# A long convolution and expert kernel: channels in four parts of 32 instead of two of 64, the first transform in fp32 on two row groups, and the spectra copied to SBUF before they are multiplied

## The chip, the cores and the metric

One core of a Trainium2 chip runs the whole program. The time is device microseconds of one execution; the number reported for a kernel is the median of several executions.

## The reference, cut to what matters

```
def _attn_ref(x, v, pos_emb, w1, w2):            # x, v: (4, 11456, 128)
    h_filt = (np.maximum(pos_emb @ w1, 0.0) @ w2) * np.exp(-0.01 * pos)[:, None]
    u = x * v
    L = 2 * S
    y = irfft(rfft(u, n=L, axis=1) * rfft(h_filt, n=L, axis=0)[None], n=L, axis=1)[:, :S]
    return x * y

def _moe_ref(x, w_skip, w_gate, w1, w2):         # x: the rows of the above, 45824 x 128
    # rows with x @ w_skip > 0 go through one of 8 experts (128 -> 1024 -> 128),
    # chosen by argmax of x @ w_gate and scaled by its softmax; the others stay x
```

So: a product of x and v, a causal convolution of 11456 positions with a filter that a small network makes, a product with x, and then for some rows one expert of eight.

## The kernel before, in words

The sequence is cut into three blocks of 3840 = 60 x 64 positions (NB = 3). Each block is transformed in two stages: a first transform of length 60 (matrix c1) and a second of length 64 (matrices c2, one for each of 60 frequencies). Spectra of the blocks of data are multiplied with spectra of the blocks of the filter, and blocks of the result get the sum of the pairs that belong to them: six products of [128, 1024] for two frequencies of 64 channels, and three sums of that size. Then c3 and c4 take the result back.

The program has four stages, in the order in which they run:

1. `first_phase` (L318). It loads x and v, multiplies them on DVE (`First.mult`, L209), splits the product into two fp32r parts (`First.split`, L215 on ACT and L216 on DVE) and multiplies them with c1 in three products of 512 columns (`First.first`, L204); ACT copies each result out of PSUM (L205), and the ACT queue stores it to the DRAM tensor x1d (L239). c1 is laid out as [120, 2, 120], half of it zeros, so that one of two positions in a tile is used per product. 25 of 48 such steps are done here, the half of the channels that comes first and one more. Between the steps runs the filter (`filt`, L244 to L315): the network, then its first transform (L290), stored to x1d by the POOL queue (L298).
2. `freq_phase` (L356). 60 iterations, each with two frequencies of 64 channels. SP loads c2 (L395) and x1 (L397). PE multiplies the filter's part with c2 (L403, tile t), ACT copies it into gc (L409, four copies), and DVE and POOL make the combined filter g from gc (L410, L411). PE multiplies the data with c2 (L428, tile xp in PSUM); DVE multiplies xp, straight from PSUM, with gc or g (`mult`, L422, six in an iteration); POOL adds the partial products (`add`, L424, three in an iteration). Two iterations later PE multiplies y with c3 (L455), ACT copies zps to z (L456), and SP stores z to the DRAM tensor zd (L460). The 23 remaining steps of the first transform are put between these by `second` and `step` (L371 to L386), in plain fp32 products. The order is written out by hand and each engine runs its instructions in that order.
3. `out_phase` (L1005). SP loads zt from zd (L1060) and a piece of x (L1049); PE multiplies zt with c4 (L1071), DVE with x (L1072), the rows are stored, routed to experts, and the first expert slots run beside this.
4. `late_slots` (L845): the rest of the expert slots.

Names that the later text uses: t, xp, zps are PSUM tiles; x1, gc, g, y, p, z, zt, ox, u and ur are SBUF tiles; in the trace, tiles of the first transform carry the name wf, since they lie in the buffer that later holds the experts' weights; `SPq` and `ACTq` are DMA queues that these engines issue to.

Of the kernel before, what the change touches and what calls it, by code (L numbers as in the profile page):

```python
# [20 lines left out]
E, F = 8, 1024  # L21
# [6 lines left out]
DH = D // 2  # L28
# [13 lines left out]
AHEAD = 1  # L42
LEAD = 3
PIECES = 1.2
FSTART = 2
FEND = 2
QX = 4
# [26 lines left out]
def tables():  # L74
# [6 lines left out]
    c1 = np.zeros((2, K1, 2, K1, 2))  # L81
    c1f = np.zeros((64, 2, 2, K1, 2))
    for p in range(2):
        c1[p, :, p] = c1f[:K1, p, p] = np.stack([np.cos(th), -np.sin(th)], axis=-1)
# [53 lines left out]
    winp = winp.transpose(1, 0, 2, 3)  # L138
    return {
        "c1": c1.reshape(2 * K1, 2, 2 * K1).astype(f), "c1f": c1f.reshape(128, 2, 2 * K1).astype(f),  # L140
        "c2": c2.astype(f), "c3": c3.astype(f),
# [14 lines left out]
class First:  # L156


    Q = 4
    STEPS = NB * N2 // (2 * Q)  # L160
    XV, US, XS = 3, 2, 3

    def __init__(self, nc, i, x1d, mc, stage):
        self.nc, self.i, self.x1d = nc, i, x1d
        n = self.Q * B * DH
        at = [0]

        def piece(k):
            at[0] += k * n
            return stage[0:2 * K1, at[0] - k * n:at[0]]  # L170
        self.xv = [[piece(1) for _ in range(self.XV)] for _ in "xv"]
        self.us = [piece(1) for _ in range(self.US)]
        self.xs = [piece(2) for _ in range(self.XS)]
        self.c1 = mc.tile([2 * K1, 2, 2 * K1], F32, name="c1")
        nc.scalar.dma_start(self.c1, i["c1"])
        self.tiles, self.loaded, self.parts = {}, 0, {}

    def halves(self, pool):
        self.c1r = pool.tile([2 * K1, 2, 2, 2 * K1], F32R, name="c1r")
        self.nc.scalar.copy(self.c1r[:, 0], self.c1)  # L180
        self.nc.vector.tensor_tensor(self.c1r[:, 1], self.c1, self.c1r[:, 0].bitcast(F32), ALU.subtract)

    def ahead(self, step):

        while self.loaded < min(step + self.XV, 2 * self.STEPS):
            self.load(self.loaded)
            self.loaded += 1

    def load(self, step):
        nc, Q = self.nc, self.Q  # L190
        h, r = divmod(step, self.STEPS)
        blk, ch = divmod(r, N2 // (2 * Q))
        self.tiles[step] = []
        for a, nm in enumerate("xv"):
            t = self.xv[a][step % self.XV]
            nc.sync.dma_start(
                t.rearrange("n (q c) -> n q c", q=Q),
                self.i[nm][ch * 2 * Q:(ch + 1) * 2 * Q, :, blk, h].rearrange("(q p) n b d -> (p n) q (b d)", p=2))
            self.tiles[step].append(t)

    def first(self, xs, terms, pool):
        ps = pool.tile([2 * K1, 512], F32, name="ps")
        for a, (c, rhs) in enumerate(terms):
            self.nc.tensor.matmul(ps, c, rhs, start=(a == 0), stop=(a == len(terms) - 1))  # L204
        self.nc.scalar.copy(xs, ps.rearrange("k (q c) -> k q c", c=B * DH))  # L205

    def mult(self, step):
        if step < 2 * self.STEPS:
            self.nc.vector.tensor_tensor(self.us[step % self.US], *self.tiles.pop(step), ALU.mult)  # L209

    def split(self, step, pool):

        u = self.us[step % self.US]
        ur = pool.tile([2 * K1, 2, self.Q * B * DH], F32R, name="ur")
        self.nc.scalar.copy(ur[:, 0], u)  # L215
        self.nc.vector.tensor_tensor(ur[:, 1], u, ur[:, 0].bitcast(F32), ALU.subtract)  # L216
        self.parts[step] = ur

    def data(self, step, pool):
        nc, Q = self.nc, self.Q  # L220
        h, r = divmod(step, self.STEPS)
        blk, ch = divmod(r, N2 // (2 * Q))
        u = self.us[step % self.US]
        xs = self.xs[step % self.XS]
        n = Q * B * DH
        ur = self.parts.pop(step, None)

        def terms(p, sl):
            if ur is None:
                return (self.c1[:, p, :], u[:, sl]),  # L230
            return [(self.c1r[:, a, p, :], ur[:, b, sl]) for a, b in ((0, 0), (0, 1), (1, 0))]
        for p in range(2):
            for hf in range(n // 512):
                sl = slice(hf * 512, hf * 512 + 512)
                qs = slice(sl.start // (B * DH), sl.stop // (B * DH))
                self.first(xs.rearrange("k (q p c) -> k q p c", q=Q, p=2)[:, qs, p], terms(p, sl), pool)
                if p or hf < n // 512 - 1:
                    yield
        nc.scalar.dma_start(  # L239
            self.x1d[h][:, :, ch * 2 * Q:(ch + 1) * 2 * Q, blk * B * DH:(blk + 1) * B * DH].rearrange("k c m d -> (k c) m d"),  # L240
            xs.rearrange("k (m c) -> k m c", c=B * DH))
        yield

    def filt(self, fc, fp, pool):  # L244
# [7 lines left out]
        c1f = fc.tile([128, 2, 2 * K1], F32, name="c1f")  # L252
# [3 lines left out]
        nc.scalar.dma_start(c1f, i["c1f"])  # L256
# [8 lines left out]
        def positions(blk, k):  # L265

            pt = fp.tile([128, P], F32, name="post", bufs=4)
            for a in range(2):
                at = blk * L + a * HALF + k
                have = max(0, min(P, S - at))  # L270
                rows = slice(a * 64, a * 64 + 64)
                if have < P:
                    nc.vector.memset(pt[rows, have:], 0.0)
                if have:
                    nc.gpsimd.dma_start(pt[rows, :have], i["post"][:, at:at + have])
            return pt
# [10 lines left out]
        def forward(ch, blk, hw, xs):  # L287
            for p in range(2):
                t = pool.tile([2 * K1, M, 2, DH], F32, name="ps")
                nc.tensor.matmul(t, c1f[:, p, :], hw, start=True, stop=True)  # L290
                nc.scalar.copy(xs[p][:, :, :, blk].rearrange("k h m d -> k m h d"), t)
                yield
            if blk < NB - 1:
                return
            for p in range(2):
                n0 = p * H2 + ch * M
                for h in range(2):
                    nc.gpsimd.dma_start(self.x1d[h][:, :, n0:n0 + M, NS * DH:].rearrange("k c m d -> (k c) m d"),  # L298
                                        xs[p][:, h].rearrange("k m s d -> k m (s d)"))
        last = iter(())  # L300
        for ch in range(H2 // M):
            xs = [fp.tile([2 * K1, 2, M, NB, DH], F32, name=f"fx{p}") for p in range(2)]
# [15 lines left out]
def first_phase(tc, fi):  # L318

    with (  # L320
# [5 lines left out]
        fi.halves(fc)  # L326
        f = fi.filt(fc, fp, fps)
        left = 0.0
        pieces = NB * 64 * H2 // 512 + 3 * NB * H2 // 4
        pace = pieces / (4 * (fi.STEPS - FSTART - FEND))  # L330
        END = fi.STEPS + AHEAD
        fi.ahead(0)

        def ready(step):
            if step < END:
                fi.mult(step)
                fi.split(step, fp)
        ready(0)
        for step in range(END):
            for n, _ in enumerate(fi.data(step, fps)):  # L340
                if n == 0:
                    fi.ahead(step + 1)
                    ready(step + 1)
# [7 lines left out]
            if step == fi.STEPS - 1:  # L351
                for _ in f:
                    pass
# [1014 lines left out]
```

## Time and profile before

| what | number |
|---|---|
| median of 3 runs | 1761.56 us (1755.21 to 1770.01) |
| the profiled execution, its own time | 1761.34 us |
| its span, first to last instruction | 1759.6 us |
| mean granted TensorE clock | 0.969 |
| busy share PE, DVE, ACT, POOL | 92%, 72%, 49%, 58% |
| moved by DMA | 357.80 MB, 203 GB/s over the span |
| first_phase | 0 to about 226 us |
| freq_phase | about 226 to 843 us |
| out_phase | about 845 to 1300 us |
| late_slots | about 1300 to 1748 us |

A row of the grouped view names line, engine, operation, what it writes and reads, shapes (partitions x elements) and count; then the busy time in us, the mean of one in ns, and the engine's idle time just before them with what ended it. A row of the view by windows gives, for a stretch of time, the busy time of each engine, the granted clock, the busy share of the 16 DMA engines and what they moved in GB/s. A row of the timeline has start and duration in us. PE runs a plain fp32 product as two instructions, so each such product counts twice in PE's rows.

### The profile page before, as it was taken

Reading aid. Unit: us, or ns where it says so; the run is one execution under the profiler, and the core shown is the slowest. Engines: PE = TensorE matmul, PEld = TensorE weight load, DVE = VectorE, ACT = ScalarE, POOL = GpSimd, SP = SyncE. Lnnn points to the kernel's source line nnn. Section 1 sums busy time; section 2 is a strip of 40 time slices with the busy share of each in tenths; the row PEclk is TensorE's granted clock in tenths of the full one; section 3 lists DMA queues with packets and bytes.
Section 4 is the critical chain, followed back from the end, with each engine's and each line's share of the span. In section 5 each row is a group of like instructions: output and inputs, shape, how many; then the busy total and the mean of one; then the engine's idle time right before and its main releaser. Section 6 shows DMA issues by size and latency. Waiting matters only on the chain. (4 is left out here: it accounts for less than half of the span.)

```text
span 1759.6 us, 27314 instructions
## 1 busy us (share of the span) xinstructions
PE 1615.1 (92%) x8980; PEld 1121.0 (64%) x8980; DVE 1269.8 (72%) x2404; ACT 862.7 (49%) x1582; POOL 1020.3 (58%) x767
## 2 busy tenths in 40 slices
PE   4989679999999799999567999999998999999996
PEld 2556345555556466655234677777677888888996
DVE  3334359777788799999277778767786777777885
ACT  3655435454454344443133555555544555556773
POOL 1111138677678699999002563632657777776874
PEclk9999889999999899999898999999998999999998
DMA  9999999999998599985999888998831111111110
GB/s 246 304 314 304 299 290 277 305 334 301 338 294 239 160 283 302 276 236 147 214 281 257 223 239 233 247 241 227 232 108 47 31 46 46 44 41 33 36 37 21
DMA packets 255122, 357.80 MB, mean 203 GB/s; under 512 B 24961, under 2 KB 189739, under 8 KB 254979
## 3 DMA queue, kind: packets, MB, share of 16 engines
q1 hardware_dynamic: 187692, 269.74, 53.2%
q10 hardware_dynamic: 47687, 47.71, 8.9%
q0 software_dynamic: 19600, 38.59, 8.4%
q8 instruction: 72, 1.18, 0.3%
q14 instruction: 71, 0.58, 0.1%
HBM read 212.91 MB, written 144.02 MB: 203 GB/s over the span
## 5 line engine op out<-in xcount | busy, mean ns | idle before, releaser
L424 POOL TENSOR_TENSOR y<-y,p 128x1024 f32<-128x1024 f32 x120 | 282.9, 2358 | 101.0 <-DVE y L422 96.3
L455 PE MATMUL zps<-y,c 128*128 128x512 f32 x720 | 339.6, 595 | 0.0
L767 POOL DMA_INDIRECT out<-o,ids x186 | 201.6, 1084 | 178.0 <-DVE o L773 128.5
L703 POOL DMA_INDIRECT xt<-out,ids x186 | 199.1, 1070 | 93.1 <-issue 42.5
L422 DVE TENSOR_TENSOR p<-xp,g 128x1024 f32<-128x1024 f32 x180 | 218.4, 1213 | 44.3 <-PE xp L428 27.0
L422 DVE TENSOR_TENSOR y<-xp,gc 128x1024 f32<-128x1024 f32 x180 | 218.5, 1214 | 20.9 <-PE xp L428 20.9
L428 PEld LDWEIGHTS xp<-x,c 128*128 128x128 f32 x720 | 137.6, 192 | 109.5 <-issue 77.2
L871 DVE SCALAR_TENSOR_TENSOR hh<-hp,hh 128x1024 fp32r<-128x1024 f32 x128 | 155.9, 1218 | 70.5 <-ACT hh L870 70.5
L428 PE MATMUL xp<-x,c 128*128 128x256 f32 x720 | 187.9, 384 | 14.1 <-DVE p L422 14.1
L455 PEld LDWEIGHTS zps<-y,c 128*128 128x128 f32 x720 | 134.9, 191 | 99.9 <-issue 89.7
L456 ACT COPY z<-zps 128x512 f32<-128x512 f32 x180 | 104.0, 587 | 189.2 <-PE zps L455 187.2
L669 POOL DMA_INDIRECT ids<-lists,at x93 | 102.7, 1104 | 134.5 <-DMA out<-xm 93.8
L409 ACT COPY gc<-t 64x384 f32<-64x384 f32 x240 | 113.7, 474 | 135.2 <-DVE y L422 80.1
L870 ACT ACTIVATE hh<-hp 128x1024 fp32r<-128x1024 f32 x128 | 132.1, 1032 | 74.2 <-PE hp L763 74.2
L205 ACT COPY wf<-ps 120x512 f32<-120x512 f32 x192 | 110.4, 591 | 83.4 <-PE ps L204 38.5
L738 DVE TENSOR_TENSOR ws<-wf,ws 128x1024 fp32r<-128x1024 f32 x113 | 137.8, 1220 | 18.1 <-ACT ws L733 11.8
L424 POOL TENSOR_TENSOR p<-p,p 128x1024 f32<-128x1024 f32 x60 | 149.5, 2492 | 0.0
L204 PE MATMUL ps<-ur,c1r 120*120 120x512 f32 x300 | 113.3, 508 | 37.9 <-ACT ur L215 20.4
L1071 PE MATMUL y<-zt,c 120*64 120x512 f32 x384 | 108.4, 643 | 32.0 <-DMA zt<-zd 25.9
L833 PEld LDWEIGHTS bank<-wd,h 128*128 128x128 f32 x928 | 107.8, 191 | 30.9 <-issue 30.8
L761 PE MATMUL hp<-hl,ws 128*128 128x512 f32 (+1 forms) x336 | 122.2, 364 | 2.4 <-DVE hh L871 0.9
L733 ACT CAST ws<-wf 128x1024 fp32r x113 | 117.8, 1043 | 10.4 <-issue 5.1
(194 smaller groups left out, 3330.8 us busy)
## 6 DMA issues: line engine op xcount, KB each, us to landing
x<-x1d SPq DMA_DIRECT2D x60, 960.0 KB
x1d<-wf ACTq DMA_DIRECT2D x48, 960.0 KB
zd<-z SPq DMA_DIRECT2D x120, 384.0 KB
zt<-zd SPq DMA_DIRECT2D x96, 480.0 KB
out<-xm SPq DMA_DIRECT2D x96, 258.0 KB
ox<-xo SPq DMA_DIRECT2D x96, 256.0 KB
wf<-x SPq DMA_DIRECT2D x48, 480.0 KB
wf<-v SPq DMA_DIRECT2D x48, 480.0 KB
```

Of the source, the lines that this page charges most:

```text
L409: nc.scalar.copy(gc[h * 64:(h + 1) * 64, a], t[a * 64:(a + 1) * 64])
L422: nc.vector.tensor_tensor(o, x[:, None].broadcast_to([128, 2, B, D]), v[:, :, None, :].broadcast_to([128, 2, B, D]), ALU.mult)
L424: add = lambda o, v: nc.gpsimd.tensor_tensor(o, o, v, ALU.add)
L428: nc.tensor.matmul(x[:, :, k], c2[:, k], x1[:, k, blk * B:(blk + 1) * B, :], start=True, stop=True)
L455: nc.tensor.matmul(zps, c3[:, a, :], y[:, blk, a], start=(a == 0), stop=(a == 1))
L703: ins = nc.gpsimd.indirect_dma_start(out=xt[:, j], out_offset=None, in_=self.rows[0:have], in_offset=bass.IndirectOffsetOnAxis(ap=ids[:, j ...
L733: nc.scalar.copy(w[:, 0], (self.w1f, self.w2f)[which][:, ds(self.where(nc.scalar, tb), F)])
L738: eng.tensor_tensor(w[:, 1], src[:, ds(self.where(eng, tb), F)], w[:, 0].bitcast(F32), ALU.subtract)
L761: nc.tensor.matmul(hp, w[:, 0, c], hl[:, 0], start=True, stop=False)
L767: ins = nc.gpsimd.indirect_dma_start(out=self.rows, out_offset=bass.IndirectOffsetOnAxis(ap=ids[:, j:j + 1], axis=0), in_=o, in_offset=Non ...
L870: nc.scalar.activation(h[:, 0], hp, AF.Relu)
L871: nc.vector.scalar_tensor_tensor(h[:, 1], hp, 0.0, h[:, 0].bitcast(F32), ALU.max, ALU.subtract)
```

## The change

The channels are cut into four parts of 32 (NP = 4), where there were two of 64.

- First transform: x and v come in one tensor xv, laid out beforehand so that a step reads one run of 6144 bytes a partition (two DMAs of 60 partitions). The tile's rows 0 to 59 and 64 to 123 hold two positions; the rows between are cleared once by six memsets. `split` and the fp32r parts are gone: two plain fp32 products of 60 rows and 384 columns, one on rows 0 to 59 of the array and one on rows 64 to 123, write two PSUM banks. c1 is [128, 120] without zeros. The result goes to x1d by the SP queue, one step late, in runs of 6144 bytes. There are 64 steps; 16 of them, one part, run in `first_phase`, and 48 in `freq_phase`.
- Filter: its first transform uses the same two row groups and is stored to a tensor of its own, x1f. The filter's positions are laid out beforehand.
- `freq_phase`: 60 iterations again, each now with four frequencies (KS) of 32 channels. c2 is loaded once, in the first 15 iterations, and stays in SBUF. x1 comes by two DMAs, the data's in runs of 1536 bytes and the filter's in runs of 384 bytes. PE makes data and filter spectra in one product of 480 columns for each frequency, four in an iteration (tile xp, four banks). ACT copies the filter's part to gc as before (four copies), and the data's part to a new SBUF tile xc (two copies). DVE multiplies xc with g: three instructions of 3072, 2048 and 1024 elements where there were six of 1024. POOL adds in two instructions, of 2048 and 1024 elements, where there were three of 1024; g is made in one POOL and one DVE instruction of 384 elements.
- zd has rows of 384 channels' worth of blocks; zt is read from it in runs of 512 bytes where they were of 1024. z is stored at a later place in the iteration.
- The experts' weights are loaded in the last 15 iterations, in another order; some small tiles and their memsets move from `freq_phase` to the start of `out_phase`.

```
-DH = D // 2
+NP = 4
+DH = D // NP
-LEAD = 3
-PIECES = 1.2
+LEAD = 4
+KS = 4
 class First:
-    Q = 4
-    STEPS = NB * N2 // (2 * Q)
+    Q = 2
+    RUN = NS * DH
+    STEPS = N2 // (2 * Q)
+    ALL = NP * STEPS
...
+        for xv in self.xv:
+            for rows in (slice(32, 64), slice(96, 128)):
+                nc.vector.memset(xv[rows], 0.0)
+        self.c1 = mc.tile([128, 2 * K1], F32, name="c1")
...
+        for p in range(2):
+            self.nc.sync.dma_start(self.xv[step % self.XV][p * 64:p * 64 + K1], self.i["xv"][h, ch, p])
...
+            rows = slice(0, 64 + K1)
+            xv = self.xv[step % self.XV][rows]
+            self.nc.vector.tensor_tensor(self.us[step % self.US][rows], xv[:, 0], xv[:, 1], ALU.mult)
...
-            return [(self.c1r[:, a, p, :], ur[:, b, sl]) for a, b in ((0, 0), (0, 1), (1, 0))]
+        for q in range(Q):
+            ps = [pool.tile([2 * K1, 512], F32, name="ps")[:, 0:RUN] for _ in range(2)]
+            for p in range(2):
+                rows = slice(p * 64, p * 64 + K1)
+                nc.tensor.matmul(ps[p], self.c1[rows], u[rows, q * RUN:(q + 1) * RUN], start=True, stop=True)
+            for p in range(2):
+                nc.scalar.copy(xs[:, 2 * q + p], ps[p])
+            if q == 0:
+                self.store()
...
 def freq_phase(...)
+        def step():
+            n = fi.STEPS * fi.Q
+            credit[0] += (n - LEAD) / (NB * (PER - QX)) if done[0] < n else n / (NB * PER)
...
-            x1 = qx.tile([128, 2, NS + NB, DH], F32, name="x1")
-            nc.sync.dma_start(x1, fi.x1d[h][ks].rearrange("k c n (s d) -> (c n) k s d", d=DH))
+            if h == 0:
+                nc.sync.dma_start(c2(ks.start, KS), i["c2"][:, ks.start * 128:ks.stop * 128])
+            x1 = qx.tile([128, KS, (NS + NB) * DH], F32, name="x1")
+            nc.sync.dma_start(x1[:, :, 0:fi.RUN], fi.x1d[h][ks].rearrange("k c n w -> (c n) k w"))
+            nc.sync.dma_start(x1[:, :, fi.RUN:], fi.x1f[ks, :, :, h * w:(h + 1) * w].rearrange("k c n w -> (c n) k w"))
...
+        def spread(n):
+            x1 = xs.pop(n)
+            xp = qpx.tile([128, KS, 512], F32, name="xp")
+            for k in range(KS):
+                nc.tensor.matmul(xp[:, k, 0:(NS + NB) * DH], c2(n % PER * KS + k), x1[:, k], start=True, stop=True)
+            for a in range(2):
+                for h in range(2):
+                    nc.scalar.copy(gc[h * 64:(h + 1) * 64, 1:, a].rearrange("p s k d -> p k s d"), ...)
+            xc = qp.tile([128, NS, KS, DH], F32, name="xc")
+            for k in range(0, KS, 2):
+                nc.scalar.copy(xc[:, :, k:k + 2].rearrange("p s k d -> p k s d"),
+                               xp[:, k:k + 2, 0:NS * DH].rearrange("p k (s d) -> p k s d", d=DH))
+            return xc
...
+            nc.gpsimd.tensor_tensor(g[:, :, 1], v[:, 1:, 1], v[:, 0:NB, 0], ALU.add)
+            nc.vector.tensor_tensor(g[:, :, 0], v[:, 1:, 0], v[:, 0:NB, 1], ALU.subtract)
...
+        def mult(o, xc, g, blk):
+            n = 2 * (NB - blk)
+            x = xc[:, blk * B:(blk + 1) * B].rearrange("p b k d -> p b (k d)")
+            v = g[:, 0:NB - blk].rearrange("p j a d -> p (j a) d")
+            nc.vector.tensor_tensor(o.rearrange("p j a b d -> p (j a) b d"), x[:, None].broadcast_to([128, n, B, D]),
+                                    v[:, :, None, :].broadcast_to([128, n, B, D]), ALU.mult)
...
+            if n + 1 < ALL:
+                xcs[n + 1] = spread(n + 1)
...
+                mult(y, xc, g, 0)
+            back(0)
+            if n < ALL:
+                mult(p1, xc, g, 1)
+            if n + 1 < ALL:
+                gs[n + 1] = filt()
+            store()
+            back(1)
+            if n < ALL:
+                nc.gpsimd.tensor_tensor(y[:, 1:], y[:, 1:], p1, ALU.add)
+                mult(p2, xc, g, 2)
+                nc.gpsimd.tensor_tensor(y[:, 2:], y[:, 2:], p2, ALU.add)
+            back(2)
...
 def out_phase(...)
-            z = ob.tile([2 * K1, 4, BW], F32, name="zt", bufs=ZT)
+            z = ob.tile([2 * K1, 2 * NP, BW], F32, name="zt", bufs=ZT)
             nc.sync.dma_start(z, zs[ch][:, :, blk * BW:(blk + 1) * BW])
```

How the orders of DVE and POOL move in `freq_phase`, one iteration and a half of each. Names: y and p are the products and partial products, xp the spectra in PSUM, xc their copy in SBUF, gc and g the filter's spectra, wf the tiles of the first transform. DVE before:

```order
154 L410 TENSOR_TENSOR g<-gc 128x256
155 L209 TENSOR_TENSOR wf<-wf 120x1024
156 L422 TENSOR_TENSOR y<-xp_1984,gc 128x1024
157 L422 TENSOR_TENSOR p_1960<-xp_1984,g 128x1024
158 L422 TENSOR_TENSOR y<-xp_2007,gc 128x1024
159 L422 TENSOR_TENSOR p_2027<-xp_2029,g 128x1024
160 L422 TENSOR_TENSOR y<-xp_2029,gc 128x1024
161 L422 TENSOR_TENSOR p_2028<-xp_2029,g 128x1024
162 L410 TENSOR_TENSOR g<-gc 128x256
163 L209 TENSOR_TENSOR wf<-wf 120x1024
```

DVE in the change, where L417 is `mult`, L409 is g and L198 is the product of x and v:

```order
118 L409 TENSOR_TENSOR g<-gc 128x3x128
119 L417 TENSOR_TENSOR p_1962<-xc,g 128x1024
120 L198 TENSOR_TENSOR wf<-wf 124x768
121 L417 TENSOR_TENSOR y<-xc,g 128x3072
122 L417 TENSOR_TENSOR p_2018<-xc,g 128x2048
123 L409 TENSOR_TENSOR g<-gc 128x3x128
124 L417 TENSOR_TENSOR p_2019<-xc,g 128x1024
125 L198 TENSOR_TENSOR wf<-wf 124x768
```

In a row of `mult` the first input was xp and is now xc; between two rows of g there were six products of 1024 elements, and there are three, of 1024, 3072 and 2048. POOL before:

```order
61 L411 TENSOR_TENSOR g<-gc 128x256
62 L424 TENSOR_TENSOR y<-y,p_1894 128x1024
63 L424 TENSOR_TENSOR p_1895<-p_1895,p_1894 128x1024
64 L424 TENSOR_TENSOR y<-y,p_1895 128x1024
65 L411 TENSOR_TENSOR g<-gc 128x256
```

POOL in the change, where L408 is g and L473 and L475 are the two sums:

```order
60 L408 TENSOR_TENSOR g<-gc 128x3x128
61 L473 TENSOR_TENSOR y<-y,p_1667 128x2048
62 L475 TENSOR_TENSOR y<-y,p_1668 128x1024
63 L408 TENSOR_TENSOR g<-gc 128x3x128
```

The three sums of 1024 elements became one of 2048 and one of 1024, behind the same instruction that makes g.

More of the change, by code (lines that the diff above doesn't have):

```diff
@@ L219, in data @@
[L219 to L230, printed above, removed]
-            return [(self.c1r[:, a, p, :], ur[:, b, sl]) for a, b in ((0, 0), (0, 1), (1, 0))]
[L232 to L241, printed above, removed]
+        h, ch = divmod(step, self.STEPS)
@@ L400, in filt @@
[L400 to L406 removed]
+            h, k = divmod(n, PER)
+            while done[0] < h * fi.STEPS * fi.Q:
+                next(todo)
+            ks = slice(KS * k, KS * k + KS)
```

312 lines of the change are left out of this document (134 added, 178 removed).

## The prediction

> **What bounds the kernel now.** I read the view by windows first, cut at the stage borders, because the page's shares are means over stages that have different limits.
>
> ```profile
> 0.00:226.00 226.00, 178.32 (x807) 108.97 (x808) 78.72 (x80) 113.26 (x187) 37.66 (x60) 0.93 0.99 293
> 242.00:500.00 258.00, 253.46 (x779) 144.48 (x778) 205.28 (x184) 126.81 (x236) 185.96 (x93) 0.99 1.00 311
> 600.00:840.00 240.00, 239.80 (x780) 143.83 (x779) 239.07 (x210) 98.69 (x191) 220.81 (x112) 1.00 0.81 240
> 855.00:1300.00 445.00, 408.34 (x3623) 282.54 (x3620) 322.05 (x1195) 215.59 (x544) 171.74 (x161) 0.97 0.89 236
> ```
>
> The columns are PE, PEld, DVE, ACT and POOL busy, then clock, DMA share and GB/s. Up to 500 us the DMA engines are full (0.99 and 1.00). From 600 to 840 us PE (239.8 of 240) and DVE (239.1) are both full, and POOL nearly so (220.8). From 855 us on PE leads. The change touches the first 845 us, and zt's reads after that.
>
> Next the groups of 600 to 840 us, a stretch without first transforms:
>
> ```profile
> L424 POOL TENSOR_TENSOR y<-y,p 128x1024 f32<-128x1024 f32 x57 | 134.3, 2357 | 19.2 <-DVE y L422 16.9
> L422 DVE TENSOR_TENSOR y<-xp,gc 128x1024 f32<-128x1024 f32 x83 | 100.4, 1210 | 0.0
> L422 DVE TENSOR_TENSOR p<-xp,g 128x1024 f32<-128x1024 f32 x82 | 99.1, 1209 | 0.0
> L424 POOL TENSOR_TENSOR p<-p,p 128x1024 f32<-128x1024 f32 x28 | 66.2, 2363 | 0.0
> L410 DVE TENSOR_TENSOR g<-gc 128x256 f32<-128x256 f32 x27 | 51.2, 1896 | 0.0
> L411 POOL TENSOR_TENSOR g<-gc 128x256 f32<-128x256 f32 x27 | 24.7, 914 | 0.0
> ```
>
> L410 is the strange row. It has a quarter of the elements of an L422 and takes 1896 ns, longer than the 1210 of L422. The two differ in where they read: L422 has one input in PSUM (xp) and one in SBUF, L410 has both inputs in SBUF. About 28.6 iterations lie in these 240 us, 8.39 us each.
>
> The spread of each such line over the whole run, as minimum, median and maximum in ns:
>
> ```profile
> L410 DVE TENSOR_TENSOR g<-gc x60: 414/1432/1918, 240.2 to 822.6; 128x256 f32<-128x256 f32 x60
> L209 DVE TENSOR_TENSOR wf<-wf x48: 1212/1220/2473, 10.3 to 514.7; 120x1024 f32<-120x1024 f32 x48
> L422 DVE TENSOR_TENSOR y<-xp,gc x180: 1206/1211/1226, 242.4 to 833.5; 128x1024 f32<-128x1024 f32 x180
> L411 POOL TENSOR_TENSOR g<-gc x60: 715/908/966, 240.3 to 824.2; 128x256 f32<-128x256 f32 x60
> L424 POOL TENSOR_TENSOR p<-p,p x60: 2344/2362/3363, 248.6 to 835.1; 128x1024 f32<-128x1024 f32 x60
> ```
>
> L422 never stretches, though POOL adds beside it all the time. L209 and L410, with two SBUF inputs, stretch by up to 1.25 and 1.5 us; so does POOL's L424, by up to 1.0. The timeline shows when (start and duration in us):
>
> ```profile
> 399.23 2.47 DVE L209 TENSOR_TENSOR wf<-wf 120x1024 f32<-120x1024 f32 x1
> ...
> 398.26 2.36 POOL L424 TENSOR_TENSOR y<-y,p 128x1024 f32<-128x1024 f32 x1 [1.97 <-DVE y L422]
> 400.57 3.35 POOL L424 TENSOR_TENSOR p<-p,p 128x1024 f32<-128x1024 f32 x1
> ...
> 623.82 2.35 POOL L424 TENSOR_TENSOR y<-y,p 128x1024 f32<-128x1024 f32 x1
> 626.13 0.91 POOL L411 TENSOR_TENSOR g<-gc 128x256 f32<-128x256 f32 x1
> ...
> 624.55 1.90 DVE L410 TENSOR_TENSOR g<-gc 128x256 f32<-128x256 f32 x1
> ```
>
> POOL's sum ends at 400.62; L209, issued during it, ends at 401.70, 1.08 later; POOL's next sum, issued during L209, ends at 403.92, 2.22 later. Likewise 626.17, then L410 at 626.45 (0.28 later), then L411 at 627.04 (0.59 later). So a DVE instruction with two SBUF inputs and a POOL sum do not run at the same time: each waits for the other's whole instruction. Waiting, each then needs about 0.14 us less than alone, since its start is already done.
>
> **The change part by part. The products.** Today six of the seven DVE instructions of an iteration read xp from PSUM and run beside POOL. In the change all of them read xc and g, both in SBUF, as does the product of x and v, of which 48 now lie in this stage. POOL's elements stay as many. So DVE and POOL, which today work side by side for 8.39 us, would take turns.
>
> Price of a turn, from the four waits above. DVE: 0.28 us for 256 elements and 1.08 for 1024, so 1.04 ns an element and 0.01 fixed: 3072, 2048, 1024 and 384 elements take 3.21 + 2.15 + 1.08 + 0.41 = 6.85 us. POOL: 0.59 for 256 and 2.22 for 1024, so 2.12 ns an element and 0.05 fixed: 2048, 1024 and 384 take 4.39 + 2.22 + 0.86 = 7.47. Together 14.32 us an iteration, the floor, if the other is always waiting when one ends. With the durations alone (DVE 414 and 1220 ns, POOL 715 and 2357 for the same sizes), as if each began after a gap, it is 7.44 + 7.90 = 15.34. The order of both engines shows little reason for a gap: while POOL adds p1, DVE has p2 ready, and while it adds p2, DVE has the next y. I take 14.6. The 48 products of 768 elements add 0.81 each, 39 us (0.95 and 46 at most). The stage from its first product to its last sum: 60 x 14.6 + 39 = 915 us, between 60 x 14.32 + 39 = 898 and 60 x 15.34 + 46 = 966.
>
> Today these two ends are:
>
> ```profile
> 241.28 1.23 DVE L422 TENSOR_TENSOR p<-xp,g 128x1024 f32<-128x1024 f32 x1 [0.61 <-POOL g L411]
> ...
> 837.54 2.36 POOL L424 TENSOR_TENSOR y<-y,p 128x1024 f32<-128x1024 f32 x1
> ```
>
> That is 241.3 to 839.9, 598.6 us.
>
> What lies under the 915 us, and would come out if the turns went away:
>
> ```profile
> L455 PE MATMUL zps<-y,c 128*128 128x512 f32 x720 | 339.6, 595 | 0.0
> L204 PE MATMUL ps<-wf,c 120*120 120x512 f32 x184 | 89.9, 596 | 1.9 <-ACT wf L205 1.8
> L409 ACT COPY gc<-t 64x384 f32<-64x384 f32 x240 | 113.7, 474 | 135.2 <-DVE y L422 80.1 <-PE t L403 35.5 <-PE zps L455 9.3
> L456 ACT COPY z<-zps 128x512 f32<-128x512 f32 x180 | 104.0, 587 | 189.2 <-PE zps L455 187.2 <-ACT gc L409 0.4
> L870 ACT ACTIVATE hh<-hp 128x1024 fp32r<-128x1024 f32 x128 | 132.1, 1032 | 74.2 <-PE hp L763 74.2
> ```
>
> PE streams the same columns as before (4 x 480 = 1920, before 6 x 256 + 2 x 192), in fewer instructions; c3's products stay. At most 60 x 8.39 = 503 us. Of the first transform, L204 gives 89.9 / 184 = 0.49 us a half, 0.98 for 512 columns, so 0.73 for 384: 96 pairs are 70 us if the two row groups run at once, 141 if not (no row shows it). PE needs 573 to 644 of 915. ACT: 4 x 0.474 + 3 x 0.587, two copies to xc of 768 elements between the rows of 512 and 1024, 0.81 each, and 3.2 copies of 384 at 0.47: 6.8 of 14.6 us. xc has two buffers and y three, so PE and ACT work an iteration ahead, and no product stands in line for them. DMA: all loads and stores from the start to zd add up to 227.8 MB, 41.2 of them in the stage before; 186.6 MB in 915 us is 204 GB/s, where 311 was reached. c2 saves 3.9 MB and the long runs some share, both worth nothing here. The 8.4 MB of weights lie in the last 15 iterations, some 218 us.
>
> **The first stage.** It does 16 of 64 steps where it did 25 of 48. Its bytes: 19 loads and 16 stores of 720 KB, 11.8 MB of filter, 3.6 of positions and constants: 41.2 MB, at today's 293 GB/s 141 us. The engines have less to do than that: the fp32r split goes (L215, L216), PE's products become 23 to 47 us beside some 95 of filter. Six memsets stand ahead of the first load and product:
>
> ```profile
> L714 DVE MEMSET xt<- 128x258 f32 x16 | 4.4, 273 | 0.2
> ```
>
> At 1.06 ns an element, 3072 elements take about 3 us; two stand ahead of the first load. I add 4 us: 145. The first product then comes at 145 + 15.3 (241.3 - 226.0) = 160. Bounds: at 311 GB/s 132 + 15 = 147; if PE's and ACT's chains show through, 180.
>
> **zt's reads.** They go from runs of 1024 to runs of 512 bytes.
>
> ```profile
> L1071 PE MATMUL y<-zt,c 120*64 120x512 f32 x384 | 108.4, 643 | 32.0 <-DMA zt<-zd 25.9 <-DVE xm L1131 2.1 <-DVE nt L1149 1.4
> zt<-zd SPq DMA_DIRECT2D x96, 480.0 KB
> q1 hardware_dynamic: 187692, 269.74, 53.2%
> q10 hardware_dynamic: 47687, 47.71, 8.9%
> ```
>
> PE waits for zt 25.9 us in all. The queues' rows give 8.9% of 16 x 1759.6 us over 47687 packets, 52.5 ns for 1000 bytes, and 79.8 ns for 1437: nearly by bytes. zt is 47.2 of the stage's 105 MB (236 GB/s x 445 us), so some 178 of its 396 us of DMA time. If a run of 512 bytes cost half, nothing is added; if it cost as much as 1024, DMA would need 574 us, 129 more than the stage has. By the nearest rows I take 12 us. The Trainium skill, DMA: Bandwidth & Descriptors, section "Why small descriptors are slow (HBM only)", counts three extra cycles for a packet of 32-byte beats; an estimate from that page is 38 cycles for two runs of 512 bytes against 35 for one of 1024, DMA time 411 of 445 us and no loss; no run here shows such reads of zd yet.
>
> **The sum**, against the profiled execution's own 1761.3 us (1.7 more than its span, and 0.2 less than the median of the three runs): the last sum comes at 160 + 915 = 1075 instead of 839.9, +235; zt +12; the tail behind the last sum and the late slots stay. 1761.3 + 247 = **2008 us**. Low ends together (147 + 898, zt 0) give 1966, high ends (180 + 966, zt 40) 2107.
>
> **The rivals.** (1) *No turns: the copy to SBUF costs DVE nothing.* For it: L422 never stretches, and the longer instructions make handing over rarer. Against it: L209 and L410 do stretch, by the length of POOL's instruction, and L424 by the length of L209. Then DMA decides: 186.6 MB at 311 GB/s, 600 us (PE 573, DVE and POOL 7.9 us an iteration at most). The last sum at 760, 80 earlier, zt +12: **1693 us**, faster. It decides if products with two SBUF inputs pass beside sums; each turn that is spared gives back up to 3.2 us. The Trainium skill speaks for this way in VectorE: DVE Perf Modes, section "Rules for kernel authors": for element-wise work on a product's output, stay with PSUM as source or copy to SBUF first if many operations follow; by that rule alone the sum would be the 1693. Its page SBUF — State Buffer, section "Who interferes with whom", speaks against the change: an instruction with two SBUF inputs and a GpSimd instruction that reads SBUF exclude each other; the trace agrees (403.92 and 401.70 above).
>
> (2) *zt becomes the bound*, a run of 512 bytes costing as much as one of 1024: 2008 - 12 + 129 = **2125 us**. Against it: the packets' cost goes by bytes, and PE leads that stage.
>
> (3) *The two row groups do not run at once*, so the change doesn't do what it says. 71 us more on PE, all under the turns: no other time under my forecast. Under (1) PE would need 644 us, and the time were 1737.
>
> **How the numbers follow.** My forecast has 86%: the waiting is in every L410 of the busy stretch. (1) has 8%, (2) 4%, some mixture near no change 2%. The predicted time is 2008 us. The range, 1955 to 2110, is the low and the high end with a little room below; it leaves out (1) and (2). Runs of this kernel spread by 0.8%, so about 1% can be told from no change: faster 0.08, within 1% 0.02, slower 0.90.
>
> **What would show it.** Right: L417 rows well over 3.4, 2.3 and 1.2 us, because their waits count in their durations; POOL's sums over 4.6 and 2.4; DVE and POOL both nearly full in this stage, PE near two thirds; some 14.6 us an iteration; DMA near 200 GB/s; a first product near 160 us. Wrong: L417 near 3.4, 2.3 and 1.2 us while POOL adds, and an iteration near 9 to 10 us with DMA at 1.0; or an out phase much longer than 445 us.

## The result and the profile after

The changed kernel takes 1998.28 us (median of four runs, 1997.51 to 2003.45), the kernel before 1759.90 us (median of four, 1755.21 to 1770.01): a ratio of 1.135, with a 95% interval from 1.130 to 1.141. The forecast was 2008 us. The profiled execution's span went from 1759.6 to 1996.1 us.

First the view by windows of the changed kernel, cut at its own stage borders: the first stage, the frequency stage with and without the last first products, the stage that reads zt. The columns are those of the prediction: PE, PEld, DVE, ACT, POOL busy, clock, DMA share, GB/s.

```profile
0.00:155.00 155.00, 110.21 (x648) 58.76 (x648) 41.67 (x52) 63.25 (x131) 21.14 (x44) 0.89 0.86 267
171.00:800.00 629.00, 499.44 (x1175) 195.96 (x1176) 624.63 (x210) 277.64 (x550) 487.81 (x124) 0.90 0.75 227
800.00:1073.00 273.00, 195.05 (x381) 81.73 (x380) 272.67 (x107) 92.06 (x168) 248.46 (x59) 0.86 0.53 146
1088.00:1536.00 448.00, 410.69 (x3620) 283.13 (x3621) 322.02 (x1195) 215.36 (x544) 172.77 (x161) 0.97 0.93 235
```

In the middle two rows DVE is busy for 624.6 of 629 and 272.7 of 273 us. PE, which was full from 600 to 840 us before, and the DMA engines, which were full up to 500 us, have room (79% and 71% of PE, 0.75 and 0.53 of DMA). A reader who stops here would call DVE the bound and look for work to take off it. The groups of the whole run, with shapes kept apart, say more:

```profile
L427 PE MATMUL zps<-y,c 128*128 128x512 f32 x720 | 404.0, 698 | 124.8 <-ACT z L428 116.9 <-POOL y L473 4.6 <-POOL y L475 3.2
L473 POOL TENSOR_TENSOR y<-y,p 128x2048 f32<-128x2048 f32 x60 | 287.3, 4789 | 68.8 <-DVE p L417 66.5 <-PE ps L215 2.3
L475 POOL TENSOR_TENSOR y<-y,p 128x1024 f32<-128x1024 f32 x60 | 277.9, 4632 | 81.5 <-DVE p L417 78.8 <-DVE first L503 1.2 <-DVE wg L976 1.2
L417 DVE TENSOR_TENSOR p<-xc,g 128x1024 f32<-128x1024 f32 x60 | 264.2, 4403 | 0.0
L417 DVE TENSOR_TENSOR y<-xc,g 128x3072 f32<-128x3072 f32 x60 | 238.8, 3980 | 2.8 <-PE zps L427 1.8 <-ACT xc L400 1.0
L417 DVE TENSOR_TENSOR p<-xc,g 128x2048 f32<-128x2048 f32 x60 | 220.3, 3671 | 0.0
```

The product of 1024 elements costs more (4403 ns) than the one of 3072 (3980). POOL's sum of 1024 (4632) costs nearly as much as that of 2048 (4789). A duration that does not follow the size has a wait inside it. What each one waits for stands in the timeline of one iteration without a first transform, start and duration in us. DVE:

```profile
894.24 5.54 DVE L417 TENSOR_TENSOR p<-xc,g 128x1024 f32<-128x1024 f32 x1
899.70 3.34 DVE L417 TENSOR_TENSOR y<-xc,g 128x3072 f32<-128x3072 f32 x1
902.97 4.43 DVE L417 TENSOR_TENSOR p<-xc,g 128x2048 f32<-128x2048 f32 x1
907.32 1.34 DVE L409 TENSOR_TENSOR g<-gc 128x384 f32<-128x384 f32 x1
908.59 5.52 DVE L417 TENSOR_TENSOR p<-xc,g 128x1024 f32<-128x1024 f32 x1
914.03 3.35 DVE L417 TENSOR_TENSOR y<-xc,g 128x3072 f32<-128x3072 f32 x1
```

POOL in the same stretch:

```profile
893.86 4.83 POOL L473 TENSOR_TENSOR y<-y,p 128x2048 f32<-128x2048 f32 x1
899.92 5.33 POOL L475 TENSOR_TENSOR y<-y,p 128x1024 f32<-128x1024 f32 x1 [1.23 <-DVE p L417]
905.21 3.04 POOL L408 TENSOR_TENSOR g<-gc 128x384 f32<-128x384 f32 x1
908.21 4.82 POOL L473 TENSOR_TENSOR y<-y,p 128x2048 f32<-128x2048 f32 x1
```

Start plus duration is the end of each. Put in one row, the ends are: p of 1024 at 899.78, y at 903.04 (3.26 later), the sum of 1024 at 905.25 (2.21 later), p of 2048 at 907.40 (2.15), POOL's half of g at 908.25 (0.85), DVE's half at 908.66 (0.41), the sum of 2048 at 913.03 (4.37), the next p of 1024 at 914.11 (1.08). The seven steps are one iteration, so they must add up to its length of 14.33 us (from one y to the next, 899.70 to 914.03); that says nothing yet. What says something is each step by itself. The p of 1024 ends 1.08 us after the sum before it, though it was issued 4.4 us before that sum ended, and 1.08 us is the time that its own work takes. So it is with every step: each is the price of one turn, as if no two instructions worked at once. They also end in the order in which they started, whichever engine they belong to; the timelines of DVE and POOL show no exception over the whole stage. The two engines do the work of one.

The ends of the stage, from the timelines of DVE and POOL:

```profile
171.18 3.36 DVE L417 TENSOR_TENSOR y<-xc,g 128x3072 f32<-128x3072 f32 x1 [1.02 <-ACT xc L400]
...
1070.72 2.34 POOL L475 TENSOR_TENSOR y<-y,p 128x1024 f32<-128x1024 f32 x1
```

So the time went here, in us, each rounded by itself:

| stretch | before | after | difference |
|---|---|---|---|
| start to the first product | 241.3 | 171.2 | -70.1 |
| first product to the last sum | 598.6 | 901.9 | +303.3 |
| last sum to the first product on zt | 14.5 | 15.4 | +0.9 |
| products on zt, start of the first to start of the last | 441.4 | 443.7 | +2.3 |
| the rest | 463.8 | 464.0 | +0.2 |

### The profile page after: what moved, and what is told of

It is laid out like the page before. It is cut to its first block, busy times and chain, and to the rows that moved or that the text cites. A ratio compares the mean times of both kernels' runs of the same rounds, so it can differ in the third digit from the quotient of the medians.

```text
span 1996.1 us, 26630 instructions
## 1 busy us (share of the span) xinstructions
PE 1660.0 (83%) x8528; PEld 1006.2 (50%) x8528; DVE 1611.1 (81%) x2220; ACT 916.8 (46%) x1740; POOL 1261.9 (63%) x691
## 5 line engine op out<-in xcount | busy, mean ns | idle before, releaser
L427 PE MATMUL zps<-y,c 128*128 128x512 f32 x720 | 404.0, 698 | 124.8 <-ACT z L428 116.9
L417 DVE TENSOR_TENSOR p<-xc,g 128x2048 f32<-128x2048 f32 x120 | 484.4, 4037 | 0.0
L473 POOL TENSOR_TENSOR y<-y,p 128x2048 f32<-128x2048 f32 x60 | 287.3, 4789 | 68.8 <-DVE p L417 66.5
L475 POOL TENSOR_TENSOR y<-y,p 128x1024 f32<-128x1024 f32 x60 | 277.9, 4632 | 81.5 <-DVE p L417 78.8
L427 PEld LDWEIGHTS zps<-y,c 128*128 128x128 f32 x720 | 147.3, 216 | 335.8 <-issue 321.5
L417 DVE TENSOR_TENSOR y<-xc,g 128x3072 f32<-128x3072 f32 x60 | 238.8, 3980 | 2.8 <-PE zps L427 1.8
L215 PE MATMUL ps<-wf,c 60*120 60x384 f32 x512 | 143.9, 601 | 104.1 <-ACT wf L217 60.5
L396 ACT COPY gc<-xp 64x384 f32<-64x384 f32 x240 | 113.7, 474 | 204.9 <-PE xp L393 118.3
L408 POOL TENSOR_TENSOR g<-gc 128x384 f32<-128x384 f32 x60 | 172.4, 2873 | 46.7 <-ACT gc L396 46.7
L198 DVE TENSOR_TENSOR wf<-wf 124x768 f32<-124x768 f32 x64 | 151.1, 2363 | 48.8 <-DMA wf<-xv 26.0
L393 PE MATMUL xp<-x,wf 128*128 128x480 f32 x352 | 160.1, 600 | 17.4 <-ACT xc L400 10.8
L400 ACT COPY xc<-xp 128x768 f32<-128x768 f32 x120 | 90.0, 802 | 156.4 <-DVE p L417 152.9
L217 ACT COPY wf<-ps 120x384 f32<-120x384 f32 x256 | 112.0, 495 | 67.9 <-PE ps L215 51.6
```

Source lines behind the costliest of these rows:

```text
L198: self.nc.vector.tensor_tensor(self.us[step % self.US][rows], xv[:, 0], xv[:, 1], ALU.mult)
L215: nc.tensor.matmul(ps[p], self.c1[rows], u[rows, q * RUN:(q + 1) * RUN], start=True, stop=True)
L393: nc.tensor.matmul(xp[:, k, 0:(NS + NB) * DH], c2(n % PER * KS + k), x1[:, k], start=True, stop=True)
L408: nc.gpsimd.tensor_tensor(g[:, :, 1], v[:, 1:, 1], v[:, 0:NB, 0], ALU.add)
L417: nc.vector.tensor_tensor(o.rearrange("p j a b d -> p (j a) b d"), x[:, None].broadcast_to([128, n, B, D]), v[:, :, None, :].broadcast_to( ...
L427: nc.tensor.matmul(zps, c3[:, a, :], y[:, blk, a], start=(a == 0), stop=(a == 1))
```

## Experiments

The theory: a DVE instruction whose inputs both lie in SBUF and a POOL instruction that reads SBUF take turns, and the copy of the spectra to SBUF (xc) brings all products under that rule. The rivals: DVE simply has too much to do in its new, wider products; or the partition of the channels, the first transform on two row groups or the wider tiles cost the time, and the stretching is only their sign.

On the chip of the first four experiments the kernel before took 1950.37 us (median of seven). The three complete variants that were profiled there needed 1095 to 1115 us behind the last sum, where the changed kernel had needed 923, so those runs are compared by their frequency stages, and by whole times only against the kernel before on the same chip.

**POOL's work moved to DVE.** The changed kernel, with POOL's half of g and both sums on DVE:

```
-            nc.gpsimd.tensor_tensor(g[:, :, 1], v[:, 1:, 1], v[:, 0:NB, 0], ALU.add)
+            nc.vector.tensor_tensor(g[:, :, 1], v[:, 1:, 1], v[:, 0:NB, 0], ALU.add)
...
-                nc.gpsimd.tensor_tensor(y[:, 1:], y[:, 1:], p1, ALU.add)
+                nc.vector.tensor_tensor(y[:, 1:], y[:, 1:], p1, ALU.add)
                 mult(p2, xc, g, 2)
-                nc.gpsimd.tensor_tensor(y[:, 2:], y[:, 2:], p2, ALU.add)
+                nc.vector.tensor_tensor(y[:, 2:], y[:, 2:], p2, ALU.add)
```

> The changed kernel with POOL's two sums and its half of g moved to DVE, the engine that is already fullest in the frequency stage (98 to 100%). Theory of turns (a DVE instruction with two SBUF inputs and a POOL sum exclude each other): the waits go, DVE alone needs 3.27 + 2.20 + 1.13 for the products, 0.94 for both halves of g and 2.20 + 1.13 for the sums, 10.9 us an iteration plus 0.87 for each of 48 first products, so 60 x 10.9 + 42 = 694 us from the first product to the last sum where the changed kernel took 902: about 1790 us, with L417 rows at 3.4, 2.3 and 1.2 us. Rival (DVE's products from SBUF are slow by themselves, or PE's and ACT's chain sets the pace): DVE gets 4.3 us more in each iteration, some 2200 us, or no change near 1998.

Its groups from 250 to 870 us, then a window inside the stage:

```profile
L417 DVE TENSOR_TENSOR y<-xc,g 128x3072 f32<-128x3072 f32 x53 | 177.5, 3349 | 0.0
L417 DVE TENSOR_TENSOR p<-xc,g 128x2048 f32<-128x2048 f32 x53 | 121.1, 2284 | 0.0
L473 DVE TENSOR_TENSOR y<-y,p 128x2048 f32<-128x2048 f32 x53 | 121.1, 2285 | 0.0
```

```profile
500.00:870.00 370.00, 325.14 (x778) 134.17 (x776) 368.64 (x252) 186.23 (x355) 0.00 (x0) 0.97 0.77 232
```

The stage goes from 173.5 to 880.3 us: 706.8 instead of 901.9, 195 us less, though an engine that the windows show as full was given all of another's work. The product of 2048 elements falls from 3671 to 2284 ns and that of 3072 from 3980 to 3349. DVE is as full as before (368.6 of 370), but now with work. That rules out too much work on DVE as the cause. The stage is 13 us over the 694 of the theory. Each sum now needs the product just ahead of it on the same engine: in the last iteration the product of 2048 ends at 875.60 and its sum starts at 875.62, where other instructions start 0.08 us before the one ahead ends. Two such places in each of 60 iterations would be some 12 us; no run tries this by itself. The whole, one run, is 1976.83 us, beside 1950.37 for the kernel before on that chip.

**The copy alone, in the kernel before.** Its channels, tiles and first transform stay; only the spectra are copied to SBUF ahead of the products:

```
-                x = x.rearrange("p b k d -> p b (k d)")
+                xc = qp.tile([128, B, D], F32, name=f"xc{blk}")
+                nc.scalar.copy(xc, x.rearrange("p b k d -> p b (k d)"))
+                x = xc
```

> The kernel before with one part of the change alone: ACT copies xp from PSUM to an SBUF tile (three copies of 512 elements an iteration) and DVE multiplies the copy; two halves of channels, fp32r split, loads and order as before. Theory of turns: six products at 1.08 and g at 0.28 on DVE, three sums at 2.22 and g at 0.59 on POOL, one after another: 14.0 us an iteration where it was 8.4 in the undisturbed part; 60 x 14.0 + 23 x 1.08 = 866 us from the first product to the last sum where it was 599: about 2028 us. Rival (the cost lies in the rest of the change: narrow runs of data, the fp32 first transform, the single xp buffer, PE's lower clock): ACT's 1.8 us more an iteration lie beside DVE, 1760 to 1780 us.

Its groups of products and sums from 600 to 1100 us, and DVE's timeline:

```profile
L422 DVE TENSOR_TENSOR y<-xc,gc 128x1024 f32<-128x1024 f32 x106 | 279.1, 2633 | 0.0
L424 POOL TENSOR_TENSOR y<-y,p 128x1024 f32<-128x1024 f32 x71 | 226.5, 3190 | 103.8 <-DVE y L422 101.2
```

```profile
709.30 3.36 DVE L422 TENSOR_TENSOR y<-xc,gc 128x1024 f32<-128x1024 f32 x1
712.58 3.36 DVE L422 TENSOR_TENSOR p<-xc,g 128x1024 f32<-128x1024 f32 x1
```

POOL's timeline in the same stretch:

```profile
708.39 3.19 POOL L424 TENSOR_TENSOR y<-y,p 128x1024 f32<-128x1024 f32 x1 [7.02 <-DVE y L422]
711.54 3.32 POOL L424 TENSOR_TENSOR p<-p,p 128x1024 f32<-128x1024 f32 x1
```

A window late in its stage, without first transforms:

```profile
840.00:1100.00 260.00, 191.88 (x513) 109.04 (x514) 260.00 (x128) 96.17 (x187) 209.57 (x74) 0.86 0.51 143
```

One run: 2216.94 us, 266.6 more than the kernel before on that chip; the frequency stage, from 237.7 to 1112.0, takes 874.3 us. Both are within 10 us of the expectation (267, and a stage of 866). Ends again stand in a row: the sum at 711.58, the product at 712.66, the next sum at 714.86, the next product at 715.94. These are steps of 1.08, 2.20 and 1.08, the turn prices that the prediction read from L209 and L410. In the window DVE is full and PE at 74%, much as in the changed kernel; ACT, which makes the added copies, is busy for 96 of the 260 us. So the operand's place alone, with ACT's copy that puts it there, brings the loss, without any of the other edits.

**POOL writes only.** The changed kernel with clears of p1 and p2 in place of the two sums. The partial products are not added, so only its stage is read, not its total.

```
-                nc.gpsimd.tensor_tensor(y[:, 1:], y[:, 1:], p1, ALU.add)
+                nc.gpsimd.memset(p1, 0.0)
                 mult(p2, xc, g, 2)
-                nc.gpsimd.tensor_tensor(y[:, 2:], y[:, 2:], p2, ALU.add)
+                nc.gpsimd.memset(p2, 0.0)
```

> The changed kernel with POOL's two sums replaced by clears of the same partial-product tiles (2048 and 1024 elements): the partial products are not added, POOL only writes in their place, and every wait between the engines stays. To be read from the frequency stage alone, since the routing of rows later depends on the data. Theory of turns, if it is the reading that excludes: the products run at 3.4, 2.3 and 1.2 us beside the clears, and the stage falls from 902 to 600 to 640 us, set by data movement or PE. If any POOL instruction on SBUF excludes DVE: the products stretch by the length of each clear. Rival (PE's and ACT's chain sets the pace, POOL only waits): the stage stays near 900 us, with DVE idle in place of waiting inside its instructions.

Its groups from 250 to 700 us, and two rows of the timelines of POOL and DVE:

```profile
L417 DVE TENSOR_TENSOR y<-xc,g 128x3072 f32<-128x3072 f32 x42 | 141.0, 3358 | 64.1 <-PE zps L427 62.4 <-POOL p L475 1.7
L473 POOL MEMSET p<- 128x2048 f32 x42 | 75.6, 1801 | 0.0
```

```profile
605.74 1.81 POOL L473 MEMSET p<- 128x2048 f32 x1
...
606.54 1.21 DVE L417 TENSOR_TENSOR p<-xc,g 128x1024 f32<-128x1024 f32 x1
```

The product of 1024 elements starts at 606.54, in the middle of a clear that lasts until 607.55, and takes 1.21 us, its time alone. In the timelines of the whole stage 44 of these products overlap a clear and not POOL's half of g, and each takes 1.21 us; 15 overlap that half of g, which reads SBUF, and take 2.02 or 2.03 us. The stage, from 168.5 to some 797, is about 629 us. DVE is not full any more and waits for PE. So it is not the presence of a POOL instruction that stops DVE, nor its writing: a clear, which reads nothing, does not exclude. How far a POOL sum waits for its reads and how far for its writes is not separated by this; and since the clears are shorter than the sums (1.80 and 0.95 us), the stage's length says less than the single overlapping rows.

**Products from PSUM in the changed kernel.** All of the change stays but xc: the data spectra lie in one PSUM bank for each frequency, three in turn, the filter's spectra in a bank of their own, and DVE multiplies from PSUM, in 12 products an iteration (four each of 768, 512 and 256 elements). Both halves of g are on POOL. Cut to its core:

```
-            xc = qp.tile([128, NS, KS, DH], F32, name="xc")
-            for k in range(0, KS, 2):
-                nc.scalar.copy(xc[:, :, k:k + 2].rearrange("p s k d -> p k s d"),
-                               xp[:, k:k + 2, 0:NS * DH].rearrange("p k (s d) -> p k s d", d=DH))
...
+                xp = qpx.tile([128, fi.RUN], F32, name="xp", bufs=3)
+                nc.tensor.matmul(xp, c2(n % PER * KS + k), xs[n][:, k, 0:fi.RUN], start=True, stop=True)
...
-            nc.vector.tensor_tensor(g[:, :, 0], v[:, 1:, 0], v[:, 0:NB, 1], ALU.subtract)
+            nc.gpsimd.tensor_tensor(g[:, :, 0], v[:, 1:, 0], v[:, 0:NB, 1], ALU.subtract)
```

> The changed kernel with its four parts, xv layout, two row groups, c2 on chip and 384-column products, but DVE multiplies straight from PSUM again: the filter's spectra have a bank of their own (four products of 96 columns), the data's spectra three banks in turn, one for each frequency; twelve products of 768, 512 and 256 elements an iteration; both halves of g on POOL; no xc. Theory of turns: only the 48 first products still take turns; DVE needs 7.2 us an iteration and 1 to 3 for a first product, PE 8.5 and 1.1, POOL 8.9; 186.6 MB at 311 GB/s are 600 us. The stage comes to 600 to 650 us, the whole to 1690 to 1760 us, below both kernels. Rival (the rest of the change costs the time): at least 1900 us.

A window over its stage, then two of its groups from 250 to 700 us:

```profile
168.00:787.00 619.00, 609.76 (x2021) 296.68 (x2021) 515.98 (x792) 291.88 (x597) 549.20 (x241) 1.00 0.93 295
```

```profile
L422 DVE TENSOR_TENSOR y<-xp,g 128x768 f32<-128x768 f32 x172 | 163.2, 949 | 52.5 <-PE zps L432 46.7 <-POOL g L411 4.5 <-PE xp L403 1.1
L490 POOL TENSOR_TENSOR y<-y,p 128x2048 f32<-128x2048 f32 x43 | 194.9, 4533 | 48.9 <-DVE p L422 36.0 <-PE zps L432 11.7 <-PE ps L215 1.1
```

The spread of the same two over the whole run, as minimum, median and maximum in ns:

```profile
L422 DVE TENSOR_TENSOR y<-xp,g x240: 940/948/960, 168.7 to 780.7; 128x768 f32<-128x768 f32 x120
L490 POOL TENSOR_TENSOR y<-y,p x60: 4507/4535/4562, 175.7 to 782.4; 128x2048 f32<-128x2048 f32 x60
```

The stage takes 620.6 us (168.7 to 789.3), 281 less than with xc, though DVE issues 12 products an iteration instead of three. Busy shares alone would not show that the engines run side by side, since a wait inside an instruction counts as busy; the spreads do. Over the whole stage neither this product nor this sum ever stretches: the one stays within 20 ns, the other within 55. PE is full (609.8 of 619) at a clock of 1.00. The whole is 1895.02 us (median of four) beside 1950.37 on that chip, a ratio of 0.971 (0.966 to 0.977). The 1690 to 1760 us that were expected were reckoned from the first chip's times and were missed on this one, and the runs (1884 to 1906 us) reach the rival's "at least 1900"; it is the stage and the ratio that decide for the theory. The stage is some 22 us longer than the 598.6 of before, and the first product comes about 70 us earlier.

**The change once more**, as it is, in a second set on another chip, where the kernel before took 1757.23 us (median of seven):

> The changed kernel as it is, once more, on the chip of this set, so that the other runs have it beside them. Theory of turns: the frequency stage is set inside the core, by DVE and POOL, so it takes 902 us from the first product to the last sum here too, within 5, whatever the stages behind it take on this chip; about 238 us above the kernel before on the same chip. Rival (data movement or PE's clock sets the stage): it moves with the chip, by 10 us or more.

The first product of DVE's timeline and the last sum of POOL's:

```profile
170.34 3.36 DVE L417 TENSOR_TENSOR y<-xc,g 128x3072 f32<-128x3072 f32 x1 [1.02 <-ACT xc L400]
...
1069.73 2.34 POOL L475 TENSOR_TENSOR y<-y,p 128x1024 f32<-128x1024 f32 x1
```

The stage is 901.7 us, the whole 1998.84 (two runs), the ratio 1.136 (1.131 to 1.142): the same as at first. That the frequency stages of the first four experiments may be set beside this one rests on the PSUM variant, whose stage took 620.6 us on their chip and, with the edit of the next experiment in its first stage, 619.6 on this one.

**Position tiles earlier.** The first product had come 11 us later than forecast. PE's timeline of the changed kernel shows waits for the position tiles in the first stage:

```profile
37.36 2.05 PE L259 MATMUL fa<-post,fw 128*128 128x512 f32 x2 [7.20 <-DMA post<-post]
...
55.61 2.04 PE L259 MATMUL fa<-post,fw 128*128 128x512 f32 x2 [5.95 <-DMA post<-post]
```

In the variant with products from PSUM, seven of them are asked for ahead instead of three:

```
-            pt = fp.tile([128, P], F32, name="post", bufs=4)
+            pt = fp.tile([128, P], F32, name="post", bufs=8)
...
-        posts = [positions(*pc) for pc in pieces[:3]]
+        posts = [positions(*pc) for pc in pieces[:7]]
...
-            if n + 3 < len(pieces):
-                posts.append(positions(*pieces[n + 3]))
+            if n + 7 < len(pieces):
+                posts.append(positions(*pieces[n + 7]))
```

> The kernel that multiplies from PSUM, with one more edit in the first stage: seven of the filter's position tiles are loaded ahead in place of three (eight buffers in place of four). Why: in the changed kernel PE stood for 7.2 and 6.0 us in the first stage until position tiles landed, with the first transforms queued behind, and DMA was busy only 0.72 of 40 to 80 us. Theory (this stall is what put the first product at 169 to 171 us where 160 was predicted): it comes to 156 to 163 us, and the whole 6 to 13 us lower, about 0.965 of the kernel before. Rival (the stage is bound by data movement over its whole length): the loads only move, the first product stays at 166 us or later.

The window of 40 to 80 us and the first product, without the edit:

```profile
40.00:80.00 40.00, 33.97 (x206) 17.38 (x206) 9.07 (x12) 18.40 (x38) 6.22 (x12) 0.86 0.71 202
```

```profile
168.73 0.96 DVE L422 TENSOR_TENSOR y<-xp,g 128x768 f32<-128x768 f32 x1 [12.15 <-POOL g L411]
```

And with it:

```profile
40.00:80.00 40.00, 37.43 (x270) 20.78 (x270) 12.03 (x16) 21.83 (x45) 3.18 (x6) 0.96 0.85 275
```

```profile
162.37 0.96 DVE L422 TENSOR_TENSOR y<-xp,g 128x768 f32<-128x768 f32 x1 [12.08 <-POOL g L411]
```

In the same 40 us DMA moves 275 instead of 202 GB/s, and the first product comes 6.4 us earlier. The two ran on different chips, but the chip does not make this difference: without the edit the changed kernel has 204 and 208 GB/s in this window and its first product at 171.2 and 170.3 us in its two profiles, the second on the chip of this run, and the variant with clears has 205 GB/s and 168.5 us. So the edit is worth 6 to 9 us at the first product. The whole does not show it by itself, since the ratio of 0.971 without it lies within the interval of the one with it. This version takes 1705.79 us (median of four, 1703.05 to 1707.69), 0.969 of the kernel before on its chip (0.966 to 0.973): it is faster than that kernel and than the change.

## Why the prediction was right

The result, 1998 us, is 10 below the forecast of 2008 and inside the range of 1955 to 2110. By its own steps:

- **The turns.** Right in mechanism. An iteration of 14.6 us was forecast, between 14.32 and 15.34; it took 14.33, the floor. The seven prices from the four waits of before (3.21, 2.22, 2.15, 0.86, 0.41, 4.39, 1.08) met 3.26, 2.21, 2.15, 0.85, 0.41, 4.37, 1.08. What the 14.6 allowed for, gaps at the handover, does not occur. The first products were under-priced: an iteration with one of them mostly takes 15.21 us, 0.88 more, where 0.81 was taken. 60 x 14.33 + 48 x 0.88 are the 902 us of the stage, instead of 915.
- **The first stage.** The sum's largest miss upward: the first product came at 171.2, not 160, though inside the bounds of 147 and 180. The bytes were right (155 us at 267 GB/s are 41.4 MB, where 41.2 were forecast); the rate was not. The step "the engines have less to do than that" failed: less work did not mean that PE was never late, since its position tiles came late and the loads behind were late with it. Asking for them earlier gave 6 to 9 of the 11 us back; the rest stays open.
- **zt's reads.** 12 us were taken, 2.3 came, though the stage's DMA share rose from 0.89 to 0.93. PE goes on leading there, and its waits for zt hardly move (25.9 us before), as the changed kernel's groups show:

```profile
L1062 PE MATMUL y<-zt,c 120*64 120x512 f32 x384 | 110.4, 654 | 33.4 <-DMA zt<-zd 24.9 <-DVE tcum L581 2.4 <-DVE oh L1109 1.7
```

- **The sum.** Of the three misses, -13, +11 and -10 us, the first two nearly cancel. So a total that is off by only 10 us, half a per cent, is in part luck; the mechanism of the turns, which gives the 303 us of the stage, is not.
- **What would show it.** L417, POOL's sums and DVE's share came as said, and DMA moved 227 and 146 GB/s in the stage's two windows, 202 over both, beside 204. PE was to be near two thirds and is at 79% and 71%: the same products took longer (L427 698 ns, before 595), at a granted clock of 0.90 and 0.86 where it had been 0.99 and 1.00.

The rivals. (1) *No turns, 1693 us*: refuted by the stretched L417 and by the copy alone, which costs 267 us. A DVE product of 1024 elements takes 1210 ns with one input in PSUM (L422 of before) and 1220 with both in SBUF when nothing excludes it (L209 of before), so the copy gains DVE nothing, and beside POOL it adds the waits. With that rival falls, for this kernel, the second choice in the rule of the Trainium skill, VectorE: DVE Perf Modes, section "Rules for kernel authors", to copy a product's output to SBUF first if many operations follow. SBUF — State Buffer, section "Who interferes with whom", of the Trainium skill says that a DVE instruction with two SBUF inputs contends with a GpSimd instruction that reads SBUF and not with one that only writes it; the traces agree, for the sums (a product of 1024 at 4403 ns) and for the clears (1.21 us). (2) *zt the bound, 2125 us*: refuted by 443.7 us against 441.4. (3) *The two row groups do not run at once*: PE's timeline shows one pair of the changed kernel's first transform between products of 512 columns (each product is two rows here, its halves):

```profile
503.30 1.88 PE L427 MATMUL zps<-y,c 128*128 128x512 f32 x4
505.11 0.91 PE L215 MATMUL ps<-wf,c 60*120 60x384 f32 x4
505.95 1.98 PE L427 MATMUL zps<-y,c 128*128 128x512 f32 x4
```

The four halves of a pair, 384 columns each, take 0.91 us, and the four halves of two products of 512 columns take 1.88. One after another the halves of the pair would need 4 x 384 / 512 x 0.47 = 1.41 us, so the two row groups do run at once; 0.73 us a pair was forecast.

## What to carry to other kernels

Before a tensor_tensor operand is moved from PSUM to SBUF, look at what POOL does at that time: beside POOL's sums the PSUM operand is what lets both engines run here, and the turns can be priced beforehand from the few instructions with two SBUF inputs that the old trace has. An engine that a profile shows as 99% busy may be waiting inside its instructions; the sign is one form of instruction with durations far apart, or a small one that takes longer than a large one. When the work of a stage shrinks, check what was asked for in time only because the stage was long.

## What the runs showed of the hardware that was not expected

- The exclusion has no gap and no loss: 14.32 us computed as the plain sum of turns, 14.33 measured. An instruction that waits its turn needs about 0.14 us less than alone once it gets it.
- The turn goes by the order of starting, not back and forth between the engines: y starts at 899.70, just before DVE's p ends at 899.78, and so comes ahead of POOL's sum, which starts at 899.92 and has to wait until y ends at 903.04.
- POOL's clears ran beside products with two SBUF inputs without stretching them (1.21 us for 1024 elements, 44 times).
- The granted clock was lower where PE had more to wait: 0.86 in the copied kernel of before (from 840 us on) and 0.86 to 0.90 in the changed one, against 0.97 with the sums on DVE and 1.00 with the products from PSUM. The runs show the two together, not which brings the other.
